# A spectral transformer block: moving the first stage's statistics, corrections, low parts and shift sums between engines

## The chip, the cores and the metric

The kernel runs on one core of one Trainium2 chip. A core has the matrix engine TensorE (PE in the profile, its weight loads PEld), VectorE (DVE), ScalarE (ACT), GpSimd (POOL) and SyncE (SP, which here only issues transfers), each with its own queue of instructions worked off in order, and 16 DMA engines. The metric is device time in microseconds (us) of one execution. A kernel's time is the median of several runs; the profile is of one execution.

## The reference, cut to what matters

```python
mod = (_silu(c) @ w_mod).reshape(c.shape[0], 6, 1, -1)
sa, ca, ga, sb, cb, gb = (mod[:, 0], mod[:, 1], mod[:, 2], mod[:, 3], mod[:, 4], mod[:, 5])
h = _layernorm(x, axis=-1) * (1 + ca) + sa
x = x + ga * _A_ref(h, A_w_r, A_w_i)      # rfft2 over (2048, 512), times complex weights, irfft2
h = _layernorm(x, axis=-1) * (1 + cb) + sb
x = x + gb * _B_ref(h, B_w1, B_b1, B_w2)  # 512 -> 1376, Mish, 1376 -> 512
```

`x` is 1 x 2048 x 512 in float32, `c` is 1 x 512, `w_mod` 512 x 3072. `ca` is called the scale here and `sa` the shift; both are sums over the 512 rows of `w_mod`.

## The kernel before

The 2048 rows are 16 tiles of 128 partitions; tile n holds the rows with index n modulo 16. Three stages follow one another: the forward transform along both axes (the *first stage*, lines 274 to 340), the products with the spectral weights (line 521 on), and the inverse transform with the two dense layers (line 694 on). The order of the instructions on every engine is the order of the program text, written out by hand (`tc.manual_schedule()`). The change is almost wholly in the first stage.

**Start of the first stage.** TensorE runs 14 products of ones (`warm`, L272). ScalarE's queue loads `c` and the scale's part of `w_mod` (`wmc`, two transfers of 512 KB, L277), SP's queue everything else: the transposed tile `xring`, the constants `kr`, the tile `x` and the column matrices `mraw` of tile 0, and then the same three for each tile. The scale sums (`scale_sums`, L238) are 16 products of `wmc` with the gated `c`, in two halves with 4 more warming products between them. VectorE makes the scaled row constants `krs` from them (`scale_rows`, L243, four instructions). The row products with ones give `kb` (`row_sums`, copied by ScalarE at L207), which takes the mean out later.

**Per tile n.** Layernorm's division is put off until after the row transform:

- `norm_sums` (VectorE, L107 and L108): mean and variance of the tile.
- `p1_scale`, for two tiles at a time: epsilon is added on VectorE (L113), ScalarE makes a first guess of the reciprocal root by a logarithm and an exponential (L114, L115), and four small instructions correct it by one Newton step (L129 to L132), on GpSimd except for the first tiles.
- `p1_split`: ScalarE rounds the column matrix to its high part (L188), GpSimd subtracts for the low part (L189) and negates the imaginary halves (L190). It runs three tiles ahead.
- `p1_row` (TensorE, L196): the row products of the transposed tile with `krs`, two tiles ahead of the column products.
- `p1_mean`: VectorE takes the mean out (L211), ScalarE scales by the reciprocal root and rounds (the high part `gh`, L213).
- `p1_low` (VectorE, L219): the low part `gl`, the scaled tile minus `gh`.
- `p1_col` (TensorE, L227 to L229): three trios of products, matrix high x `gh`, matrix low x `gh`, matrix high x `gl`.
- `p1_save` (ScalarE, L233): the result leaves its bank.

The buffers of `gh` and `gl` (tags `g1`, `g2`) are two each, those of the mean-free tile two for each parity, and those of tag `t` two.

**End of the first stage.** The shift sums (`shift_sum`, L248 and L250) run at tiles 10 to 13: ScalarE scales one part of `wms`, GpSimd adds it up. Before the last column product TensorE turns the sum into columns (`mod_columns`, L99); after it come the shift's row products (`shift_rows`, L259) and then the next stage's transposes (L424).

Later stages use `norm_stats` and `norm_scale` for the second layernorm, with the same guess and correction (`norm_refine`, L118 to L124, all on VectorE).

Of the kernel before, what the change touches and what calls it, by code (L numbers as in the profile page):

```python
# [26 lines left out]
def tile_spectral_block(ctx: ExitStack, tc: tile.TileContext, x_d, w1_d, b1_d, w2_d,  # L27
# [40 lines left out]
    nmr = base.tile([P, N2], F32, name="nmr")  # L68

# [40 lines left out]
    def norm_guess(lo, hi):  # L110
        ve = small.tile([P, 4], F32, name="ve")[:, 0:hi - lo]
        r = rstd[:, lo:hi]
        nc.vector.tensor_scalar(ve, mv[:, lo:hi, 1], EPS, None, op0=ALU.add)  # L113
        nc.scalar.activation(r, ve, AF.Ln)  # L114
        nc.scalar.activation(r, r, AF.Exp, scale=-0.5)  # L115
        return ve

    def norm_refine(lo, hi, ve):  # L118
        r = rstd[:, lo:hi]
        nc.vector.tensor_tensor(ve, ve, r, op=ALU.mult)  # L120
        nc.vector.tensor_tensor(ve, ve, r, op=ALU.mult)
        nc.vector.tensor_scalar(ve, ve, -0.5, 1.5, op0=ALU.mult, op1=ALU.add)
        nc.vector.tensor_tensor(r, r, ve, op=ALU.mult)
        nc.vector.scalar_tensor_tensor(nmr[:, lo:hi], mv[:, lo:hi, 0], -1.0, r, op0=ALU.mult, op1=ALU.mult)  # L124

    def p1_scale(lo, hi, eng):
        ve = norm_guess(lo, hi)
        r = rstd[:, lo:hi]
        eng.tensor_tensor(ve, ve, r, op=ALU.mult)  # L129
        eng.tensor_tensor(ve, ve, r, op=ALU.mult)  # L130
        eng.tensor_scalar(ve, ve, 0.5, -1.5, op0=ALU.mult, op1=ALU.add)
        eng.tensor_tensor(r, r, ve, op=ALU.mult)  # L132

    def norm_scale(lo, hi):
        norm_refine(lo, hi, norm_guess(lo, hi))
# [73 lines left out]
    def p1_mean(n):  # L209
        c = buf("hy"[n % 2])  # L210
        nc.vector.scalar_tensor_tensor(c, kb, mv[:, n, 0:1], st.pop(("pg", n)), op0=ALU.mult, op1=ALU.subtract)  # L211
        gh = buf("g1", F32R)
        nc.scalar.activation(gh, c, AF.Copy, scale=rstd[:, n:n + 1])  # L213
        st["g", n] = c, gh

    def p1_low(n):
        c, gh = st.pop(("g", n))
        gl = buf("g2", F32R)
        nc.vector.scalar_tensor_tensor(gl, c, rstd[:, n:n + 1], plain(gh), op0=ALU.mult, op1=ALU.subtract)  # L219
        st["g", n] = gh, gl  # L220
# [25 lines left out]
    def shift_sum(k):  # L246
        t = macc if k == 0 else buf("t")
        nc.scalar.activation(t, wms[:, k, :], AF.Copy, scale=sc[:, k:k + 1])  # L248
        if k:
            nc.gpsimd.tensor_tensor(macc, macc, t, op=ALU.add)  # L250

# [22 lines left out]
    with tc.manual_schedule():  # L274
# [21 lines left out]
        for k in range(4):  # L296
            scale_sums((k,), cps)
            if k == 1:
                warm(4)
# [583 lines left out]
```

## Time and profile before

| what | before |
|---|---|
| runs | 414.62, 415.5, 417.48 us; median 415.5 |
| profiled execution | 414.65 us, of which span 412.7 us |
| TensorE clock granted | 0.999 of full, mean |
| busy, share of the span | PE 96%, PEld 83%, DVE 47%, ACT 35%, POOL 21% |
| first stage | about 0 to 60 us |

The span is what the profile shows; about 2 us of the execution lie around it. A timeline row gives the start, the duration, the engine, the line, the operation, what it writes and reads, the tile's shape and, in brackets, how long the engine stood idle before it and what ended that. "x8" is a merged run of like instructions. A row of one line's instructions gives the count and the shortest, median and longest duration in ns, and the first and last start. A row of waits gives who waited for whom, microseconds in total, how many times and the longest. Matmuls are pipelined: the start of the next says more than the duration. A matmul in float32 stands as two instructions.

### The profile page before, as it was taken

Reading aid. Unit: us, or ns where it says so; the run is one execution under the profiler, and the core shown is the slowest. Engines: PE = TensorE matmul, PEld = TensorE weight load, DVE = VectorE, ACT = ScalarE, POOL = GpSimd, SP = SyncE. Lnnn points to the kernel's source line nnn. Section 1 sums busy time; section 2 is a strip of 40 time slices with the busy share of each in tenths; the row PEclk is TensorE's granted clock in tenths of the full one; section 3 lists DMA queues with packets and bytes.
Section 4 is the critical chain, followed back from the end, with each engine's and each line's share of the span. In section 5 each row is a group of like instructions: output and inputs, shape, how many; then the busy total and the mean of one; then the engine's idle time right before and its main releaser. Section 6 shows DMA issues by size and latency. Waiting matters only on the chain.

```text
span 412.7 us, 5968 instructions
## 1 busy us (share of the span) xinstructions
PE 397.7 (96%) x2287; PEld 343.1 (83%) x2287; DVE 192.1 (47%) x377; ACT 146.3 (35%) x322; POOL 87.6 (21%) x139
## 2 busy tenths in 40 slices
PE   8799979999999999899999999999999999999996
PEld 8798867999899998688878888878888878888874
DVE  2798847787337697553421442311432312422213
ACT  2466844667734752633411222310232310111110
POOL 0467745666214354312100000000000000000000
PEclk9999999999999999999999999999999999999999
DMA  8999790464302223111000200000200000200002
GB/s 294 378 355 320 210 302 6 128 219 162 97 6 83 76 63 87 49 51 29 18 0 2 102 0 2 0 2 0 102 2 0 0 2 0 102 2 1 0 2 102
DMA packets 20316, 34.59 MB, mean 84 GB/s; under 512 B 3648, under 2 KB 6496, under 8 KB 19904
## 3 DMA queue, kind: packets, MB, share of 16 engines
q1 hardware_dynamic: 19856, 33.16, 24.3%
q10 hardware_dynamic: 432, 1.05, 0.7%
q8 instruction: 18, 0.29, 0.3%
q14 instruction: 10, 0.08, 0.1%
HBM read 30.01 MB, written 4.19 MB: 83 GB/s over the span
## 4 chain that ended last, share of the span: by engine, by line
PE 87%; DVE 4%; POOL 3%; issue 2%; ACT 1%; DMA 1%; POOLq 0%
PE bank L664 30%; PE bank L685 29%; PE bank L627 4%; PE bank L617 4%; PE bank L618 3%; PE bank L440 3%; PE bank L486 3%; PE bank L593 2%; PE bank L473 2%; PE bank L272 2%; PE bank L424 1%; PE bank L196 1%; POOL mring L189 1%; DVE buf L456 1%; POOL mring L190 1%
## 5 line engine op out<-in xcount | busy, mean ns | idle before, releaser
L685 PE MATMUL bank<-w,ah 128*128 128x512 f32 (+1 forms) x352 | 108.7, 390 | 1.4 <-issue 1.4
L664 PE MATMUL bank<-h,w1h 128*128 128x512 f32 (+1 forms) x352 | 96.8, 398 | 0.0
L672 ACT ACTIVATE mw<-bank,b1n 128x512 f32<-128x512 f32 (+1 forms) x44 | 30.2, 688 | 181.6 <-PE bank L664 129.1
L673 DVE CAST ah<-mw 128x512 fp32r<-128x512 f32 (+1 forms) x44 | 20.1, 457 | 156.9 <-ACT mw L672 156.9
L685 PEld LDWEIGHTS bank<-w,ah 128*128 128x128 f32 (+1 forms) x352 | 66.1, 188 | 16.1 <-issue 1.8
L664 PEld LDWEIGHTS bank<-h,w1h 128*128 128x128 f32 (+1 forms) x352 | 65.0, 187 | 15.1
L685 PE MATMUL bank<-w,al 128*128 128x512 f32 (+1 forms) x176 | 68.6, 390 | 0.0
L664 PE MATMUL bank<-h,w1l 128*128 128x512 f32 (+1 forms) x176 | 48.2, 396 | 0.0
L664 PEld LDWEIGHTS bank<-h,w1l 128*128 128x128 f32 (+1 forms) x176 | 32.9, 187 | 8.1
L685 PEld LDWEIGHTS bank<-w,al 128*128 128x128 f32 (+1 forms) x176 | 33.0, 188 | 7.4 <-DVE al L674 0.4
L674 DVE TENSOR_TENSOR al<-mw,ah 128x512 fp32r<-128x512 f32 (+1 forms) x44 | 30.4, 692 | 4.5 <-DVE ah L673 0.5
L227 PE MATMUL bank<-buf,mring 128*128 128x512 f32 x48 | 20.8, 433 | 6.4 <-ACT buf L213 3.9
L617 PE MATMUL bank<-kc,d 128*128 128x128 f32 x128 | 24.8, 276 | 0.5 <-ACT d L349 0.5
L618 PE MATMUL bank<-kc,d 128*128 128x128 f32 x128 | 24.7, 275 | 0.0
L107 DVE BATCH_NORM_STATS2 st<-x 128x6 f32<-128x512 f32 x32 | 22.0, 687 | 3.2 <-DMA x<-in_A_x_dram 2.8
L640 POOL TENSOR_TENSOR buf<-buf,modr 128x512 f32<-128x512 f32 (+1 forms) x11 | 14.2, 1287 | 33.5 <-DMA buf<-in_B_w_dram 27.8
L573 POOL TENSOR_TENSOR w1l<-buf,w1h 128x512 fp32r<-128x512 f32 (+1 forms) x12 | 14.4, 1201 | 27.3 <-ACT w1h L572 27.3
L617 PEld LDWEIGHTS bank<-kc,d 128*128 128x128 f32 x128 | 19.4, 192 | 0.7 <-ACT d L349 0.7
L618 PEld LDWEIGHTS bank<-kc,d 128*128 128x128 f32 x128 | 19.4, 192 | 0.0
L189 POOL TENSOR_TENSOR mring<-mraw,mring 128x256 fp32r<-128x256 f32 x16 | 13.9, 867 | 18.0 <-ACT mring L188 18.0
L627 PE MATMUL bank<-kiv,buf 128*128 128x128 f32 x128 | 17.2, 277 | 0.0
L196 PE MATMUL bank<-modr,xring 128*128 128x128 f32 x128 | 16.9, 276 | 0.0
(141 smaller groups left out, 550.0 us busy)
## 6 DMA issues: line engine op xcount, KB each, us to landing
buf<-in_B_w_dram SPq DMA_DIRECT2D x18, 256.0 KB, 2.7
xring<-in_x_t_dram SPq DMA_DIRECT2D x16, 256.0 KB, 5.0
x<-in_A_x_dram SPq DMA_DIRECT2D x16, 256.0 KB, 5.3
wm<-in_w_mod_dram SPq DMA_DIRECT2D x16, 256.0 KB, 4.4
out_dram<-x SPq DMA_DIRECT2D x16, 256.0 KB, 2.1
mraw<-in_km_dram SPq DMA_DIRECT2D x16, 128.0 KB, 5.0
wqa<-in_w_q_dram SPq DMA_DIRECT2D x8, 256.0 KB, 4.3
wqb<-in_w_q_dram SPq DMA_DIRECT2D x8, 256.0 KB, 5.6
```

The lines of the kernel that those rows point to most:

```text
L107: nc.vector.bn_stats(t, x[:, n, :])
L189: nc.gpsimd.tensor_tensor(m[:, 1, 0:256], mraw[:, n, :], plain(m[:, 0, 0:256]), op=ALU.subtract)
L196: nc.tensor.matmul(pgv[:, j], data(j), krs[:, j, :].rearrange("p (c q) -> p c q", c=2), start=True, stop=True)
L227: nc.tensor.matmul(pa, m[:, a, 0:128], g, start=(i == 0), stop=False)
L617: nc.tensor.matmul(o, dj[:, 0:128], kc[0][:, n, :], start=True, stop=False)
L618: nc.tensor.matmul(o, dj[:, 64:192], kc[1][:, n, :], start=False, stop=True)
L627: nc.tensor.matmul(px[:, j * P:(j + 1) * P], e[:, j * P:(j + 1) * P], kiv[:, j, :], start=True, stop=True)
L664: nc.tensor.matmul(ps, w[:, k, fs], h[:, k, :], start=(i == 0), stop=(i == 11))
L672: nc.scalar.activation(w, ps, AF.Mish, bias=b1n[:rows, g % NF:g % NF + 1])
L673: nc.vector.tensor_copy(ah, w)
L674: nc.vector.tensor_tensor(al, w, plain(ah), op=ALU.subtract)
L685: nc.tensor.matmul(out_ps[b][j], a[:, j * P:(j + 1) * P], w2[f // 6][:rows, f % 6, w, :], start=(f == 0 and i == 0), stop=(f == NF - 1 and ...
```

## The change

Line numbers in this section and the diff are the changed kernel's own where they are new.

- The scale's part of `w_mod` is loaded in four transfers of 256 KB: parts 1 and 3 on ScalarE's queue, parts 0 and 2 on SP's, after the transposed tile 0 and ahead of `kr` and tile 0's `x`. The warming products before the scale sums are 11 instead of 14, and the 4 between their halves are gone.
- Tile 0's statistics stand after the scale sums in the text; on VectorE they are ahead of the scaled row constants, as before, but its correction comes after these.
- Epsilon comes in as ScalarE's bias in the logarithm (a tile `eps`), so L113 goes. The correction is three `scalar_tensor_tensor` instructions instead of four, all on VectorE, in the later stages too (where the fifth, for `nmr`, stays).
- Statistics run four tiles ahead of the column products instead of three, and the guess and the correction of a pair are split: the guess at odd n, the correction at the next even n, between the mean step of tile n + 1 and the low part of tile n.
- Odd tiles: ScalarE scales into a plain tile of tag `t`, copies that to `gh`, and GpSimd subtracts for `gl`. Even tiles stay as they were (VectorE makes `gl`).
- The shift sums are four VectorE instructions (`mod_step`), two at n = 12 and two at n = 13; the columns are taken before column product 14 instead of 15.

On VectorE the order of an even n in the steady part is: mean step of n + 1, three correction steps for n + 2 and n + 3, low part of n, statistics of n + 4; of an odd n: mean step of n + 1, statistics of n + 4. On GpSimd an even n has the odd low part of n + 1, then the split of n + 3. On ScalarE an odd n ends with the guess, after the saving of n - 1, the high part of n + 1 and the split of n + 3.

```diff
     def norm_guess(lo, hi):
-        ve = small.tile([P, 4], F32, name="ve")[:, 0:hi - lo]
         r = rstd[:, lo:hi]
-        nc.vector.tensor_scalar(ve, mv[:, lo:hi, 1], EPS, None, op0=ALU.add)
-        nc.scalar.activation(r, ve, AF.Ln)
+        nc.scalar.activation(r, mv[:, lo:hi, 1], AF.Ln, bias=eps)
         nc.scalar.activation(r, r, AF.Exp, scale=-0.5)
...
+    def norm_refine(lo, hi, sign):
         r = rstd[:, lo:hi]
...
+        t = small.tile([P, 4], F32, name="ve")[:, 0:hi - lo]
+        for out, a, one, op in ((t, mv[:, lo:hi, 1], EPS, ALU.add), (t, t, -0.5 * sign, ALU.mult),
+                                (r, t, 1.5 * sign, ALU.add)):
+            nc.vector.scalar_tensor_tensor(out, a, one, r, op0=op, op1=ALU.mult)
...
     def p1_mean(n):
         c = buf("hy"[n % 2])
         nc.vector.scalar_tensor_tensor(c, kb, mv[:, n, 0:1], st.pop(("pg", n)), op0=ALU.mult, op1=ALU.subtract)
-        gh = buf("g1", F32R)
-        nc.scalar.activation(gh, c, AF.Copy, scale=rstd[:, n:n + 1])
-        st["g", n] = c, gh
+        one = rstd[:, n:n + 1]
+        if n % 2:
+            g, c = c, buf("t")
+            nc.scalar.activation(c, g, AF.Copy, scale=one)
+        gh, gl = buf("g1", F32R), buf("g2", F32R)
+        if n % 2:
+            nc.scalar.copy(gh, c)
+            nc.gpsimd.tensor_tensor(gl, c, plain(gh), op=ALU.subtract)
+        else:
+            nc.scalar.activation(gh, c, AF.Copy, scale=one)
...
-        for k in (0, 2):
-            nc.scalar.dma_start(wmc[:, k:k + 2, :], wm_d[:, 1, k:k + 2, :])
+        load_scale(nc.scalar, 1)
+        load_scale(nc.scalar, 3)
         nc.scalar.preload_act_table_set("natural_log_exp_and_others")
         load_xt(0)
+        load_scale(nc.sync, 0)
+        load_scale(nc.sync, 2)
         nc.sync.dma_start(kr, kr_d)
...
-        warm(14)
-        norm_sums(0)
-        p1_scale(0, 1, nc.vector)
+        warm(11)
         cps = [bank(t) for t in "DDCC"]
         for k in range(4):
             scale_sums((k,), cps)
-            if k == 1:
-                warm(4)
+        norm_sums(0)
+        norm_guess(0, 1)
         scale_rows(cps)
+        norm_refine(0, 1, -1)
...
         norm_sums(1)
-        p1_scale(1, 2, nc.gpsimd)
         p1_mean(0)
+        norm_guess(1, 2)
+        norm_refine(1, 2, -1)
         p1_split(1)
+        p1_mean(1)
+        p1_low(0)
         p1_split(2)
+        norm_sums(2)
+        norm_sums(3)
+        norm_guess(2, 4)
         for n in range(N2):
...
-            if n + 1 < N2:
+            if 1 <= n and n + 1 < N2:
                 p1_mean(n + 1)
-            p1_low(n)
-            if n == N2 - 1:
+            if n and n % 2 == 0 and n + 2 < N2:
+                norm_refine(n + 2, n + 4, -1)
+            if n:
+                p1_low(n)
+            if n == N2 - 2:
                 shift_columns()
             p1_col(n)
             if n + 3 < N2:
                 p1_split(n + 3)
+            if n + 4 < N2:
+                norm_sums(n + 4)
             if n == 0:
-                norm_sums(2)
-            if n + 3 < N2:
-                norm_sums(n + 3)
-                if n % 2 == 0:
-                    p1_scale(n + 2, n + 4, nc.gpsimd if n else nc.vector)
-            if 10 <= n < 14:
-                shift_sum(n - 10)
+                norm_refine(2, 4, -1)
+            if n % 2 and n + 3 < N2:
+                norm_guess(n + 3, n + 5)
+            if n in (12, 13):
+                for k in (2 * n - 24, 2 * n - 23):
+                    mod_step(macc, wms[:, k, :], k, nc.vector)
```

More of the change, by code (lines that the diff above doesn't have):

```diff
@@ L68, in tile_spectral_block @@
     nmr = base.tile([P, N2], F32, name="nmr")
+    eps = base.tile([P, 1], F32, name="eps")
     saz = base.tile([P, NQ], F32, name="saz")
@@ L244, in scale_rows @@
                                            op0=ALU.mult, op1=ALU.add)
[L246 to L250, printed above, removed]
     def shift_columns():
@@ L285, in tile_spectral_block @@
         nc.vector.memset(ones, 1.0)
+        nc.vector.memset(eps, EPS)
         nc.vector.memset(b1n[:, NF - 1:NF], 0.0)
```

31 lines of the change are left out of this document (12 added, 19 removed).

## The prediction

> **What bounds the kernel now.** I read the page's engine table first, then who waited for whom on TensorE in the first stage (0 to 62 us), then the timeline of that stage, engine by engine.
>
> ```profile
> span 412.7 us, 5968 instructions
> PE 397.7 (96%) x2287; PEld 343.1 (83%) x2287; DVE 192.1 (47%) x377; ACT 146.3 (35%) x322; POOL 87.6 (21%) x139
> ...
> PE bank L227 <- ACT buf L213: 3.9, 6, 2.1
> PE bank L227 <- DVE buf L219: 2.5, 2, 2.3
> ```
>
> TensorE is busy 96% of the span, so a change can only win where it waits. Those waits stand in the first stage, at the column products (L227), behind the scaled tile (L213) and its low part (L219). The change touches that stage, so I take its clock on TensorE.
>
> ```profile
> 16.79 1.05 PE L196 MATMUL bank<-modr,xring 128*128 128x128 f32 x8
> ...
> 21.63 1.05 PE L196 MATMUL bank<-modr,xring 128*128 128x128 f32 x8
> 22.44 0.47 PE L227 MATMUL bank<-buf,mring 128*128 128x512 f32 x1
> ...
> 23.93 1.05 PE L196 MATMUL bank<-modr,xring 128*128 128x128 f32 x8
> 24.74 0.47 PE L227 MATMUL bank<-buf,mring 128*128 128x512 f32 x1
> ...
> 27.11 0.48 PE L227 MATMUL bank<-buf,mring 128*128 128x512 f32 x1
> ...
> 28.60 1.05 PE L196 MATMUL bank<-modr,xring 128*128 128x128 f32 x8
> ...
> 49.48 1.05 PE L196 MATMUL bank<-modr,xring 128*128 128x128 f32 x8
> ...
> 56.65 1.05 PE L99 MATMUL bank<-ones,modr 128*128 128x1 f32 x8 [0.39 <-POOL modr L250]
> 57.56 0.48 PE L227 MATMUL bank<-buf,mring 128*128 128x512 f32 x1
> ...
> 59.95 2.27 PE L424 MATMUL bank<-ident,a_sb 128*128 128x128 f32 x15
> ```
>
> Every column product is followed at once by the row product (L196) two tiles on, so the start of that row is the column's end. One column product takes 22.44 to 23.93 = 1.49 us (three trios), a row product 0.81 to the next column. Two tiles without a stall take 27.11 - 22.44 = 4.67. Column 4 ends at 28.60 and column 12 at 49.48: four pairs in 20.88, or 5.22 each, so 0.55 of stall per pair. From column 12 to the transposes of the next stage (59.95) are 10.47 us, with work for 0.81 + 3 x 1.49 + 0.91 (L99) + 0.90 (shift rows, 59.95 - 57.56 - 1.49) = 7.1. The next stages have full TensorE, so I let whatever the transposes gain reach the end.
>
> **The start.**
>
> ```profile
> GB/s 294 378 355 320 210 302 6 128 219 162 97 6 83 76 63 87 49 51 29 18 0 2 102 0 2 0 2 0 102 2 0 0 2 0 102 2 1 0 2 102
> ...
> 6.44 1.95 PE L238 MATMUL bank<-sc,wmc 128*128 128x128 f32 x16
> ...
> 7.53 0.69 DVE L107 BATCH_NORM_STATS2 st<-x 128x6 f32<-128x512 f32 x1 [2.79 <-DMA x<-in_A_x_dram]
> 8.22 1.05 PE L272 MATMUL bank<-ones 128*128 128x128 f32 x8
> ...
> 9.12 1.95 PE L238 MATMUL bank<-sc,wmc 128*128 128x128 f32 x16
> ...
> 10.44 1.18 DVE L243 SCALAR_TENSOR_TENSOR modr<-kr,bank 128x128 f32<-128x128 f32 x4 [0.23 <-PE bank L238]
> ...
> 13.09 0.59 ACT L207 COPY modr<-bank 128x512 f32<-128x512 f32 x1 [3.70 <-PE bank L196]
> ...
> 13.71 1.40 DVE L211 SCALAR_TENSOR_TENSOR buf<-modr,mv,bank 128x512 f32<-128x512 f32 x2 [1.08 <-ACT modr L207]
> ...
> 14.49 0.72 ACT L213 ACTIVATE buf<-buf,rstd 128x512 fp32r<-128x512 f32 x1 [0.47 <-DVE buf L211]
> ```
>
> Today TensorE runs 14 warming products, half of the scale sums (6.44), 4 warming products, and the other half (9.12); the scaled constants follow 1.32 behind. The change takes out 3 + 4 warming products; four of them take 9.12 - 8.22 = 0.90, so the scale sums would start 0.68 earlier, at 5.76. A half takes 8.22 - 6.44 = 1.78, so the second would start at 7.54 and L243's successor at 8.86, if the data are there. The four parts go two on each queue, and on SP's queue parts 0 and 2 stand ahead of kr and tile 0's x. First rows, parts, kr and x are 7 x 0.26 = 1.84 MB. By the page's slices of 10.3 us (294 and 378 GB/s) 3.03 MB have passed at 10.3, so 1.84 MB at about 7.2. Today x landed at 7.53 with weights still to come; now all of them go ahead of it or beside it. I take 8.1, an estimate between 7.5 and 9.4; the parts themselves are ahead of kr and x and then in time for TensorE. VectorE's queue now has tile 0's statistics (0.72 + 0.18) ahead of the scaled constants (27.73 to 28.45 below, and its own 0.18), so x sets them: 9.05. From there to the first mean is 13.71 - 10.44 = 3.27, which gives K = 12.3; I take 12.4 for the correction steps now behind the constants. The two more issues on SP's queue come ahead of every later load; these are spaced by the transfers, whose bytes are the same, so they cost nothing more. Gain 1.3 (bounds 0, if x lands at 9.4, and 1.6, if TensorE sets it).
>
> **VectorE, GpSimd and ScalarE per pair.**
>
> ```profile
> 26.40 0.71 DVE L211 SCALAR_TENSOR_TENSOR buf<-modr,mv,bank 128x512 f32<-128x512 f32 x1
> 27.06 0.75 DVE L219 SCALAR_TENSOR_TENSOR buf<-buf,rstd 128x512 fp32r<-128x512 f32 x1
> 27.73 0.69 DVE L107 BATCH_NORM_STATS2 st<-x 128x6 f32<-128x512 f32 x1
> 28.45 0.18 DVE L108 BATCH_NORM_AGGREGATE mv<-st 128x2 f32<-128x6 f32 x1
> 28.67 0.26 DVE L113 TENSOR_SCALAR ve<-mv 128x2 f32<-128x2 f32 x1
> 28.84 0.74 DVE L211 SCALAR_TENSOR_TENSOR buf<-modr,mv,bank 128x512 f32<-128x512 f32 x1
> ...
> 30.88 0.18 DVE L108 BATCH_NORM_AGGREGATE mv<-st 128x2 f32<-128x6 f32 x1
> 30.98 0.71 DVE L211 SCALAR_TENSOR_TENSOR buf<-modr,mv,bank 128x512 f32<-128x512 f32 x1
> ```
>
> VectorE works without a gap here: 30.98 - 26.40 = 4.58 a pair. The change takes out one low part (0.67) and the epsilon addition (0.17), and adds three correction steps. Without these it needs 2 x 0.66 (means) + 0.67 + 2 x 0.72 + 2 x 0.10 (statistics) = 3.63. What the three cost depends on who else is in the memory:
>
> ```profile
> 18.24 0.73 POOL L189 TENSOR_TENSOR mring<-mraw,mring 128x256 fp32r<-128x256 f32 x1
> 18.32 0.67 DVE L129 TENSOR_TENSOR ve<-ve,rstd 128x2 f32<-128x2 f32 x1 [0.51 <-ACT rstd L115]
> 19.03 0.16 DVE L130 TENSOR_TENSOR ve<-ve,rstd 128x2 f32<-128x2 f32 x1
> 19.06 0.41 POOL L190 TENSOR_SCALAR mring<-mring 128x256 fp32r<-128x256 f32 x1
> 19.22 0.27 DVE L131 TENSOR_SCALAR ve<-ve 128x2 f32<-128x2 f32 x1
> ...
> L573 POOL TENSOR_TENSOR w1l<-buf,w1h x12: 932/1274/1611, 121.1 to 156.9; 128x512 fp32r<-128x512 f32 x8, 128x352 fp32r<-128x352 f32 x4
> L189 POOL TENSOR_TENSOR mring<-mraw,mring x16: 722/736/1199, 9.5 to 51.0; 128x256 fp32r<-128x256 f32 x16
> L190 POOL TENSOR_SCALAR mring<-mring x16: 405/407/809, 10.3 to 52.3; 128x256 fp32r<-128x256 f32 x16
> ```
>
> A step of 0.16 on two columns, with two operands in SBUF, took 0.67 and ended 0.02 after GpSimd's operation did; the next slipped in, and the third ended with GpSimd's next one. So a correction costs 3 x 0.19 = 0.57 beside an idle GpSimd, and about 1.1 beside a busy one (rest of one operation, one short operation, 0.3 of its own). GpSimd will be busy: it loses four steps of 0.2 and gets the odd tile's low part, 1.27 by the median of L573, the same form: 1.27 + 2 x (0.74 + 0.41) + five gaps of 0.08 = 4.0 a pair, and what it waits itself comes on top. I take 1.1, so VectorE's pair is 3.63 + 1.1 = 4.73 against TensorE's 4.67; the bounds are 4.20 and 5.8 (a correction that starts with the 1.27 ahead of it). ScalarE gets one more copy per pair, 0.59 by the nearest row (13.09); TensorE waits for it only through the chain that follows. Two waits are new in queues: GpSimd's subtraction waits for ScalarE's copy with the split of three tiles on behind it, which has three tiles of time; ScalarE's logarithm waits for the second tile's statistics with the next column's saving behind it, which frees a bank of two. Statistics four tiles ahead want x sooner: a tile's three loads are 0.66 MB, 1.8 us at 378 GB/s, against 2.3 us per tile, and x of tile 4 is due 7.2 after x of tile 0, at 15.3, wanted at K+5.6 = 18.
>
> [...]
>
> **The walk through the first columns,** from K, in queue order. ScalarE ends the high part of tile 0 at K+1.5 (13.71, 14.49 and 0.72) and then has tile 1's logarithm and exponential (0.51 with the waits, by the row of 18.32; to 1.86); VectorE's correction of tile 1 waits for these, and behind it stand mean 1 (to 3.11) and low part 0 (to 3.9). So column 0 ends at K+4.5, where it took to K+3.1 before (16.79): statistics have moved, but one wait is new. The odd low part on GpSimd (ScalarE's scale and copy to 4.53, then 1.27) is there at 5.85, and column 1 ends at K+6.9 (21.63, K+7.9, before). Then statistics 2, 3 (to 5.6), 4 (6.4), correction 2-3 (7.2), mean 2 and its high part: column 2 starts at K+8.7, as before. Statistics 5, mean 3, correction 4-5 (10.45) and low part 2 (11.2) end column 2 at K+11.8 (before K+10.2); column 3 at 14.1; statistics 6 and 7, means 4 and 5, correction 6-7 and low part 4 (16.0) end column 4 at K+16.6, against 28.60 - 13.71 = 14.9. Loss 1.7 (bounds 0.8 with no collision, 3.2 with three).
>
> **Columns 4 to 12:** four pairs at 4.75, 19.0 instead of 20.88. Gain 1.9 (bounds 2.2, TensorE's 4.67, and -2.4).
>
> **The end.** The shift sums leave ScalarE and GpSimd (with the 0.39 wait at L99) and become four VectorE steps of 0.7 (of L219's kind and shape), two of them ahead of mean 14 and two ahead of mean 15. From low part 12 at time e: 4 x 0.7 + 0.66 and 0.3 for one collision = e+3.8; L99 moves ahead of column 14 and waits for it, 0.91 to e+4.75, column 14 to 6.25. Mean 15, scale, copy and GpSimd's subtraction, 0.66 + 0.72 + 0.6 + 1.27 + 0.1, are ready at e+7.2, so column 15 ends at 7.75 and the transposes start at e+8.65. Column 12, whose last trio takes some 0.55, ends at e+0.55: 8.1 against 10.47. Gain 2.4 (bounds 3.3 and 1.4). The fused correction of the later stages lies beside full TensorE: 0; without that cover it would save one step of 0.2 at five places. L99's other neighbours, the memset and the bias operand cost nothing that anyone waits for.
>
> **Sum.** 1.3 - 1.7 + 1.9 + 2.4 = 3.9. The profiled execution took 414.65 (span 412.7), 0.85 under the median of 415.5 and with the fastest run: 414.65 - 3.9 = 410.75; I say 410.7.
>
> **Rivals.**
> - *No collisions.* GpSimd's gaps let the corrections through: column 4 at K+15.7, pairs at 4.67, VectorE ahead by the end: 1.3 - 0.8 + 2.2 + 3.3 = 6.0, 408.65. Against it: GpSimd is loaded 4.0 of 4.7.
> - *The steady pairs stay at 5.22,* since a correction falls behind the long subtraction: 1.3 - 1.7 + 0 + 2.4 = 2.0, 412.65.
> - *All three steps wait,* GpSimd being back ahead of the second too: one operation (0.41 to 0.73) more per correction, 0.5 with its gap, at three in the walk and four later: 3.9 - 3.5 = 0.4, 414.25. For it: 19.03 and 19.06 stand only 0.03 apart. [...]
> - *Late start.* x lands at 9.4 or later behind four parts: 2.6, 412.05. Before, x landed at 7.53.
> - *Slower: GpSimd becomes the bound* with the subtraction. At the longest it has taken, 1.61 + 2 x (1.20 + 0.81) + 0.4 = 6.0 a pair, six pairs from K+4.5 to column 12: 52.9 + 8.65 - 0.55 = 61.0, 1.1 later than before: 415.75. It turns the sign from 5.85 a pair on; typical values give 4.0.
>
> [...]
>
> **Chances.** Forecast 0.45, no collisions 0.25, pairs at 5.22 0.14, three waits 0.07, late start 0.05, GpSimd bound 0.04. The range 408.2 to 412.7 leaves out the cases at 414.25 and 415.75 and the edges. A measurement of this kernel tells about 1% (4.15 us) from no change. Faster by more than that: the free case and some six tenths of the forecast's spread, 0.52; within 1%: 0.45; slower by more: 0.03.
>
> **What would show it.** The first scaled-constant step near 9.0 and waiting for x or the statistics, not TensorE; the first mean near 12.4; column 0's last trio waiting for VectorE's low part by 1.4; correction steps of 0.16 stretched to 0.4 to 0.7; pairs of 4.7 to 4.8 at L228; L99 waiting for VectorE's shift sum; transposes near 56.1. Wrong would be corrections at 0.19 throughout (then the free case), or TensorE waiting for GpSimd's low part in most pairs.

## The result and the profile after

The changed kernel takes 414.33 us (median of 20 runs, 412.37 to 416.04), the kernel before 415.92 (20 runs, 414.62 to 417.95): a ratio of 0.995 with the interval 0.9931 to 0.9968. It is faster, by half a per cent; the forecast was 410.7 us, 1.2% under the 415.5 known at that time. Executions of one kernel lie some 3 us apart, in part along with TensorE's mean clock (last section); hence the intervals.

The profiled execution took 413.91 us. First its page, then who waited for whom on TensorE (what waits, for what: us in all, times, longest).

```profile
span 411.7 us, 5922 instructions
...
PE 397.0 (96%) x2273; PEld 342.7 (83%) x2273; DVE 192.1 (47%) x374; ACT 151.0 (37%) x326; POOL 86.0 (21%) x116
```

```profile
PE bank L228 <- DVE buf L221: 2.7, 2, 1.7
PE bank L695 <- issue: 2.4, 1, 2.4
PE bank L100 <- DVE modr L95: 1.4, 1, 1.4
PE bank L228 <- ACT buf L213: 1.2, 2, 0.8
```

The waits at the column products (L228, L227 before) are 3.9 us instead of 6.4. Two others stand beside them: one at the shift's column sums (L100; 0.4 before, at L99) and one some 115 us later at the first down product (L695; 1.4 before, at L685). Now TensorE's timeline of the first stage.

```profile
16.92 0.50 PE L228 MATMUL bank<-buf,mring 128*128 128x512 f32 x1 [1.67 <-DVE buf L221]
...
29.16 1.05 PE L188 MATMUL bank<-modr,xring 128*128 128x128 f32 x8
...
48.05 1.05 PE L188 MATMUL bank<-modr,xring 128*128 128x128 f32 x8
...
51.88 1.05 PE L100 MATMUL bank<-ones,modr 128*128 128x1 f32 x8 [1.36 <-DVE modr L95]
52.80 0.48 PE L228 MATMUL bank<-buf,mring 128*128 128x512 f32 x1
...
54.02 0.63 PE L228 MATMUL bank<-buf,mring 128*128 128x512 f32 x1
...
54.87 0.63 PE L228 MATMUL bank<-buf,mring 128*128 128x512 f32 x1
...
57.23 1.05 PE L254 MATMUL bank<-kr,cols 128*128 128x128 f32 x8
58.12 2.04 PE L434 MATMUL bank<-ident,a_sb 128*128 128x128 f32 x13
```

Row products again mark column ends: column 4 at 29.16, column 12 at 48.05, the transposes at 58.12. With K, the first mean step, from VectorE's timeline of the start (8.43 tile 0's statistics, 9.26 the scaled constants, 12.49 the first mean):

```profile
8.43 0.69 DVE L108 BATCH_NORM_STATS2 st<-x 128x6 f32<-128x512 f32 x1 [3.81 <-DMA x<-in_A_x_dram]
...
9.26 1.15 DVE L244 SCALAR_TENSOR_TENSOR modr<-kr,bank 128x128 f32<-128x128 f32 x4
...
12.49 0.75 DVE L203 SCALAR_TENSOR_TENSOR buf<-modr,mv,bank 128x512 f32<-128x512 f32 x1 [0.17 <-ACT modr L199]
```

| stretch (us) | before | forecast | after |
|---|---|---|---|
| K | 13.71 | 12.4 | 12.49 |
| K to the end of column 4 | 14.89 | 16.6 | 16.67 |
| columns 4 to 12 | 20.88 | 19.0 | 18.89 |
| column 12 to the transposes | 10.47 | 8.1 | 10.07 |
| transposes to the first down product | 108.51 | as before | 109.32 |

Three of five steps came out within 0.11 us; the last two lost 2.0 and 0.8 of the 3.9 us forecast.

What happened at the end of the stage stands on VectorE and GpSimd. VectorE first: low part 12, then the shift sums.

```profile
46.68 0.74 DVE L221 SCALAR_TENSOR_TENSOR buf<-buf,rstd 128x512 fp32r<-128x512 f32 x1
47.35 0.47 DVE L93 TENSOR_SCALAR modr<-wms,sc 128x512 f32<-128x512 f32 x1
47.85 1.85 DVE L95 SCALAR_TENSOR_TENSOR modr<-wms,sc,modr 128x512 f32<-128x512 f32 x1
...
50.28 1.54 DVE L95 SCALAR_TENSOR_TENSOR modr<-wms,sc,modr 128x512 f32<-128x512 f32 x2
```

GpSimd beside it:

```profile
47.89 1.27 POOL L211 TENSOR_TENSOR buf<-buf 128x512 fp32r<-128x512 f32 x1 [1.13 <-DMA wqa<-in_w_q_dram]
```

The first sum with two operands in SBUF takes 1.85 us, from 47.85 on, where the two at 50.28 take 1.54 together: 1.1 too much, the length of GpSimd's subtraction less a little. TensorE waits for the sums, and right after that wait its clock is halved. Busy time and granted clock (the column of 1.00 and 0.50) of two stretches:

```profile
50.13:53.55 3.42, 2.06 (x15) 1.80 (x14) 3.30 (x6) 2.14 (x4) 1.07 (x2) 1.00 0.89 293
53.55:56.96 3.41, 3.41 (x13) 3.03 (x12) 0.00 (x0) 1.06 (x3) 1.28 (x1) 0.50 0.99 330
```

For 3.41 us TensorE never idles and runs at half clock: column products follow each other at 54.87 - 54.02 = 0.85 instead of 0.47.

The second loss, in the row stage. The kernel before, GpSimd scaling the first slab of w2 (L640) and TensorE's first down product:

```profile
150.42 1.27 POOL L640 TENSOR_TENSOR buf<-buf,modr 128x512 f32<-128x512 f32 x1 [1.51 <-DMA buf<-in_B_w_dram]
...
168.46 0.70 PE L685 MATMUL bank<-w,ah 128*128 128x512 f32 x2 [1.41 <-issue]
```

The same of the kernel after, with VectorE's split of the fourth slab (L657) and tile 15's statistics (L108) behind it:

```profile
149.58 1.28 POOL L650 TENSOR_TENSOR buf<-buf,modr 128x512 f32<-128x512 f32 x1 [2.58 <-DMA buf<-in_B_w_dram]
...
150.91 1.20 DVE L121 SCALAR_TENSOR_TENSOR ve<-ve,rstd 128x4 f32<-128x4 f32 x1
...
162.31 0.69 DVE L657 TENSOR_TENSOR w<-buf,w 128x512 fp32r<-128x512 f32 x1 [0.78 <-ACT w L656]
162.91 0.69 DVE L108 BATCH_NORM_STATS2 st<-x 128x6 f32<-128x512 f32 x1
...
167.44 0.70 PE L695 MATMUL bank<-w,ah 128*128 128x512 f32 x2 [2.42 <-issue]
```

The transposes came 1.83 earlier, the first slab only 0.84, and the down product 1.02: TensorE waits 2.42 instead of 1.41. Beside it a small correction step of tiles 8 to 11 took 1.20 instead of 0.16. I took that step for the cause at first; the runs say otherwise. "First slab" means from here on GpSimd's scaling of it, which starts when its transfer has landed.

### The profile page after: what moved, and what is told of

The parts are those of the page before. It is cut to its first block, busy times and chain, and to the rows that moved or that the text cites. A ratio compares the mean times of both kernels' runs of the same rounds, so it can differ in the third digit from the quotient of the medians.

```text
span 411.7 us, 5922 instructions
## 1 busy us (share of the span) xinstructions
PE 397.0 (96%) x2273; PEld 342.7 (83%) x2273; DVE 192.1 (47%) x374; ACT 151.0 (37%) x326; POOL 86.0 (21%) x116
## 4 chain that ended last, share of the span: by engine, by line
PE 85%; DVE 8%; ACT 2%; DMA 1%; issue 1%; SPq 0%; POOL 0%; POOLq 0%
PE bank L674 30%; PE bank L695 29%; PE bank L627 4%; PE bank L637 4%; PE bank L628 3%; PE bank L450 3%; PE bank L496 3%; PE bank L603 2%; PE bank L483 2%; DMA x<-in_A_x_dram 1%; PE bank L188 1%; PE bank L434 1%; PE bank L228 1%; DVE buf L466 1%; DVE buf L203 1%
## 5 line engine op out<-in xcount | busy, mean ns | idle before, releaser
L695 PE MATMUL bank<-w,ah 128*128 128x512 f32 (+1 forms) x352 | 108.7, 390 | 2.4 <-issue 2.4
L695 PEld LDWEIGHTS bank<-w,ah 128*128 128x128 f32 (+1 forms) x352 | 66.1, 188 | 17.0 <-issue 2.8
L695 PE MATMUL bank<-w,al 128*128 128x512 f32 (+1 forms) x176 | 68.6, 390 | 0.0
L695 PEld LDWEIGHTS bank<-w,al 128*128 128x128 f32 (+1 forms) x176 | 33.0, 188 | 7.4 <-DVE al L684 0.4
L228 PE MATMUL bank<-buf,mring 128*128 128x512 f32 x48 | 21.8, 455 | 3.9 <-DVE buf L221 2.7
L108 DVE BATCH_NORM_STATS2 st<-x 128x6 f32<-128x512 f32 x32 | 22.0, 687 | 4.2 <-DMA x<-in_A_x_dram 3.8
L640 DVE TENSOR_TENSOR x<-x,bank 128x512 f32<-128x512 f32 x16 | 10.8, 674 | 13.0 <-PE bank L637 13.0
```

What stands on the lines that cost most here:

```text
L108: nc.vector.bn_stats(t, x[:, n, :])
L228: nc.tensor.matmul(pa, m[:, a, 0:128], g, start=(i == 0), stop=False)
L695: nc.tensor.matmul(out_ps[b][j], a[:, j * P:(j + 1) * P], w2[f // 6][:rows, f % 6, w, :], start=(f == 0 and i == 0), stop=(f == NF - 1 and ...
```

## The experiments

Two theories to begin with. L: a VectorE step with two operands in SBUF is held up by a GpSimd operation that runs beside it (0.67 us for 0.16 in the kernel before, at 18.32), and this is what the change pays at three places (the first stage's corrections, the shift sums, the later corrections). C: the wait at L100 brings the clock down. All runs are compared with the kernel before on the same chip; the kernel after stands at 0.995.

**Filling the wait at L100** (the kernel after):

```
             if n == N2 - 2:
+                warm(6)
                 shift_columns()
```

> The changed kernel with six more warming products between column product 13 and the shift sum's columns; their result is not used. Theory C (the clock): TensorE stood idle for 1.36 us there and then ran products of one column, and 1.6 us later its clock fell to half for 3.4 us, which stretched columns 14 and 15 from 2.98 to 4.43. If so, the six products (0.225 us each, 1.35 in all) fill the stall without delaying anything, the records show no half clock near 53 us, columns 14 and 15 take about 3.0, the transposes start near 56.7 instead of 58.12 and the time falls by about 1.4 us (some runs of the changed kernel show more than one such stretch, so it may be up to 2). Rival S (the stall alone): the half clock is chance or comes from something else; then the stretch stays, and the time is the changed kernel's.

Measured: 413.73 us, ratio 0.9916 (0.9881 to 0.995). TensorE's timeline:

```profile
51.93 1.05 PE L100 MATMUL bank<-ones,modr 128*128 128x1 f32 x8
52.85 0.48 PE L228 MATMUL bank<-buf,mring 128*128 128x512 f32 x1
...
56.00 1.05 PE L254 MATMUL bank<-kr,cols 128*128 128x128 f32 x8
56.89 1.39 PE L435 MATMUL bank<-ident,a_sb 128*128 128x128 f32 x8
```

L100 starts at the same time, and the columns behind it need 56.00 - 52.85 = 3.15 instead of 4.43: no half clock in this profile (granted 1.00 from 50.1 to 57.0), transposes 1.23 earlier, span 410.6. That fits C, but one profile does not show it. The gain in the medians is smaller and its interval touches 0.995: the profiled execution is the only one of nine with a mean clock of 1.00, the other eight have 0.995 or 0.996, and where their clock fell is not known. The eleven profiles of the kernel after and its variants say more. In five L100 waits 1.32 to 1.36 us: three fall to half clock there (column products 0.85 apart), with 10.05 to 10.07 us from column 12 to the transposes, and two do not, with 8.74 and 8.77. In the six where the wait is filled or 0.80 and less, none falls. So in these eleven the fall at this place stands only behind the long wait, and not always; it costs 1.3 us.

**The first stage's guess in PSUM:** logarithm and exponential write a bank, so that each correction step reads one operand from SBUF; the same at the other guesses and corrections.

```
+        gps = bank("D")
-        norm_guess(2, 4)
+        norm_guess(2, 4, gps)
...
-                norm_refine(2, 4, -1)
+                norm_refine(2, 4, -1, gps)
```

> The changed kernel, but in the first stage the guess of the reciprocal root from tile 1 on is written to a PSUM bank, so each correction step reads only one operand from SBUF; the result is the same. [...] Then the steps take 0.16 to 0.25 each, a correction 0.6 to 0.75 instead of about 1.1, column 4 ends near K+15.8 instead of K+16.67 (K is the first mean), pairs take 4.67 instead of 4.73, VectorE reaches the shift sums some 0.8 us earlier relative to column 12, and the transposes start 1 to 2.5 us earlier than in the changed kernel. [...]

Measured: 410.85 us, ratio 0.9845 (0.9803 to 0.9887). The correction steps of the kernel after, seven of each (shortest/median/longest ns):

```profile
L121 DVE SCALAR_TENSOR_TENSOR ve<-mv,rstd x7: 373/554/671, 19.2 to 45.7; 128x2 f32<-128x2 f32 x7
L121 DVE SCALAR_TENSOR_TENSOR ve<-ve,rstd x7: 160/160/161, 19.7 to 46.3; 128x2 f32<-128x2 f32 x7
L121 DVE SCALAR_TENSOR_TENSOR rstd<-ve,rstd x7: 252/255/256, 19.9 to 46.5; 128x2 f32<-128x2 f32 x7
```

And with the guess in PSUM:

```profile
L121 DVE SCALAR_TENSOR_TENSOR ve<-mv,bank x7: 123/156/157, 18.8 to 43.7; 128x2 f32<-128x2 f32 x7
L121 DVE SCALAR_TENSOR_TENSOR ve<-ve,bank x7: 156/157/158, 19.0 to 43.9; 128x2 f32<-128x2 f32 x7
L121 DVE SCALAR_TENSOR_TENSOR rstd<-ve,bank x7: 156/157/158, 19.1 to 44.1; 128x2 f32<-128x2 f32 x7
```

The stretch is gone, with nothing moved: the first step takes 0.156 us instead of 0.554, by the medians. Column 4 ends at K+15.09 instead of K+16.67, columns 4 to 12 take 18.34 (46.18 - 27.84), and the transposes start at 54.40. This is the free case of the prediction, made by hand; L holds for the first stage.

**The later guess in PSUM,** in the bank pool that the transposes of the next stage use too:

```
     def norm_scale(lo, hi):
-        norm_guess(lo, hi)
-        norm_refine(lo, hi, 1)
+        g = bank("D")
+        norm_guess(lo, hi, g)
+        norm_refine(lo, hi, 1, g)
```

> The changed kernel, but in the later stage (the second layernorm) the guess lies in a PSUM bank; the first stage is as in the changed kernel. [...]

Measured: 416.13 us, ratio 0.9973 (0.9943 to 1.0002). The edit made a wait of its own: the transposes of h waited 2.2 us for the bank (L604 for L121). The mean clock of this execution is 0.990, against 0.996 in the kernel after; whether it fell behind that wait is not shown. It tells nothing on L.

**The shift sums accumulated in PSUM:**

```
-                    mod_step(macc, wms[:, k, :], k, nc.vector)
+                    nc.vector.scalar_tensor_tensor(macc if k == 3 else mps, wms[:, k, :], one, mps,
+                                                   op0=ALU.mult, op1=ALU.add)
```

> The changed kernel, but the four shift steps add up in a PSUM bank and only the last writes SBUF; the result is the same. [...] Rival: the shift steps are not what the columns wait for (mean 15 and the chain to GpSimd's last subtraction are), then columns 14 and 15 only wait elsewhere and the gain is under 0.4.

Measured: 412.7 us, ratio 0.9898 (0.9862 to 0.9933). VectorE's timeline:

```profile
48.69 0.76 DVE L354 SCALAR_TENSOR_TENSOR bank<-wms,sc,bank 128x512 f32<-128x512 f32 x1
```

The sum that took 1.85 takes 0.76. From column 12 to the transposes it is 56.56 - 48.62 = 7.94 us, near the 8.1 of the prediction; L100 waits 0.53 instead of 1.36, and the column products behind it stand 0.47 apart, not 0.85. L holds for the sums.

**The later correction in the old form,** with the epsilon added on VectorE:

```
     def norm_scale(lo, hi):
-        norm_guess(lo, hi)
-        norm_refine(lo, hi, 1)
+        nc.vector.tensor_scalar(ve, mv[:, lo:hi, 1], EPS, None, op0=ALU.add)
...
+        nc.vector.tensor_tensor(r, r, ve, op=ALU.mult)
```

> The kernel after with the correction of the later stage (the row stage and the guess for each later batch) in the form of the kernel before: epsilon added on VectorE, two products, one scalar step, one product. The first stage stays fused. In the kernel after TensorE's first down product waits 2.42 us (1.41 before), and the correction of tiles 8 to 11 has steps of 0.73 and 1.20 us that start within GpSimd's L650 and L583. Theory L (these steps have two operands in SBUF and stand still beside GpSimd; it is the moment, not the form, that decides): the old form meets the same two GpSimd instructions, two of its products are stretched to 0.6 to 1.2 us again, the down product waits 2.0 to 2.6 and the time stays at that of the kernel after, within 0.5 us (ratio 0.995 to 0.997). Rival F (the fused form itself is what costs: three steps of two operands in a row instead of two): the stretch falls below 0.7 us in sum, the wait goes back to 1.4 and the kernel is 1.0 us faster than the kernel after (ratio 0.9925).

Measured: 412.93 us, ratio 0.9888 (0.987 to 0.9906): the expectation of L missed, and its rival F (the form itself costs, 0.9925) is the nearer one. In its profile the steps ran at 0.16 each and the down product waited 1.01. From the transposes to the down product are 108.10 us, as in the kernel before (108.51) and not as in the kernel after (109.32). The traces show what the form does, ahead of the first slab of w2, where VectorE and GpSimd each subtract with two operands in SBUF (GpSimd's row is two instructions). The kernel before:

```profile
146.29 2.62 POOL L573 TENSOR_TENSOR w1l<-buf,w1h 128x352 fp32r<-128x352 f32 x2 [1.42 <-ACT w1h L572]
146.46 1.31 DVE L609 TENSOR_TENSOR h<-buf,h 128x512 fp32r<-128x512 f32 x1
```

The kernel after:

```profile
144.28 0.69 DVE L619 TENSOR_TENSOR h<-buf,h 128x512 fp32r<-128x512 f32 x1
144.30 2.70 POOL L583 TENSOR_TENSOR w1l<-buf,w1h 128x352 fp32r<-128x352 f32 x2 [1.43 <-ACT w1h L582]
```

Before, GpSimd starts first and VectorE is stretched, 1.31 for 0.69. After, the fused corrections have made VectorE 0.35 earlier against the transposes (86.16 behind them instead of 86.51). It starts 0.02 ahead of GpSimd, and GpSimd's first subtraction takes 1.46 instead of 0.94. The transfer of the first slab is issued when that one is over: 87.67 us behind the transposes instead of 87.30. This holds in every profile but that of the run with the wait for a bank. The four with the old later correction take 2.61 or 2.62 for the two subtractions and have the first slab at 90.1 to 90.5; the nine with the fused one take 2.68 to 2.70 and have it at 91.1 to 92.4. The issue stands at 87.30 and 87.32 in two of the four (the kernel before, the old later correction), and at 87.66 or 87.67 in four of the nine (the kernel after, the first run of three edits together, the split behind the statistics, the three edits that held).

**The guess of tiles 8 to 11 alone, in a free bank:**

```
+        g = bank("C") if lo == 8 else None
```

> The kernel after with the guess of tiles 8 to 11 alone (the correction with the steps of 0.73 and 1.20 us) in a PSUM bank that nothing else uses at that time (tag C, not D, which the transposes of the batches needed in the run before). Theory L (a step with one operand in SBUF does not wait for GpSimd): all three steps take 0.16 to 0.2 us, the chain behind them comes 1.5 us earlier, the down product waits 0.9 to 1.5 us instead of 2.42, and the time is 1.0 us below that of the kernel after: 413.3 beside 414.3, ratio 0.9925. Rival E (the wait of the down product comes from the activation chain behind it, ACT's table load, Mish and the cast beside GpSimd, and not from the correction): the steps take 0.16 and the wait stays above 2.2 us, the time stays (ratio 0.995).

Measured: 414.76 us, ratio 0.9933 (0.9911 to 0.9955): no gain that can be told. VectorE's timeline:

```profile
148.85 0.16 DVE L121 SCALAR_TENSOR_TENSOR ve<-mv,bank 128x4 f32<-128x4 f32 x1 [0.52 <-ACT bank L114]
...
149.43 1.19 DVE L127 SCALAR_TENSOR_TENSOR nmr<-mv,rstd 128x4 f32<-128x4 f32 x1
```

The three steps take 0.16 each, and the next step with two SBUF operands takes 1.19 in their place; the down product waits 2.16 (2.46 in the run with the filled wait, whose transposes start at the same time).

**Three edits together** (first guess, sums, tiles 8 to 11):

> Three edits in one: the guess of the first stage in PSUM, the shift sums accumulated in PSUM, and the guess of tiles 8 to 11 in PSUM. The first alone gave 0.9845, the second alone 0.9898, against 0.995 for the kernel after. Theory L, if the gains lie at different places and reach the end: pairs of 4.6 us (as with the first alone), the last stretch of the first stage 7.4 to 8.0 us from column 12 to the transposes, the down product's wait 0.9 to 1.6; in sum 2.6 + 0.7 + 1.0 below the kernel after with the first alone counted once: 409.0 us, ratio 0.979 to 0.982. Rival B (what the first stage gains is given back where TensorE waits in the later stage, because that chain is bound by transfers and not by TensorE): the down product waits 2.5 us or more and the time stays at that of the first alone, 410.8, ratio 0.984.

Measured: 412.0 us, ratio 0.9874 (0.9855 to 0.9894). The transposes start at 54.86, the corrections are nearly free, and the down product waits 2.66: rival B. So the stretch of these steps is not what holds it. GpSimd's first slab in this run:

```profile
146.65 1.27 POOL L659 TENSOR_TENSOR buf<-buf,modr 128x512 f32<-128x512 f32 x1 [2.93 <-DMA buf<-in_B_w_dram]
```

Here stood the clue. From this start to the down product (164.43) are 17.78 us; in the kernel before 168.46 - 150.42 = 18.04, after 167.44 - 149.58 = 17.86. Over the ten profiles with this order of the stage (the run with the wait for a bank left out) it is 17.72 to 18.04, while the stretch of the corrections in between goes from 0.06 to 2.1 us. What differs is when the first slab has landed: 90.1 to 92.4 us behind the transposes, and that goes with the form of the later correction (above).

**One part undone: odd low parts on VectorE as the even ones.**

```
-        if n % 2:
-            nc.scalar.copy(gh, c)
-            nc.gpsimd.tensor_tensor(gl, c, plain(gh), op=ALU.subtract)
-        else:
-            nc.scalar.activation(gh, c, AF.Copy, scale=one)
+        nc.scalar.activation(gh, c, AF.Copy, scale=one)
```

> One part of the change undone: the low parts of odd tiles are made as those of even tiles, by one fused step on VectorE (L221) instead of a second copy on ScalarE and a subtraction on GpSimd. The pairs of columns 4 to 12 then load VectorE with one step of 0.74 us more: in the kernel after VectorE is busy 18.07 of 18.89 us there, or 4.5 of 4.72 a pair. Theory D (VectorE's own work sets the pair; the move to GpSimd is what made the pair 4.7): pairs of 5.2 to 5.4 us, columns 4 to 12 in 21 instead of 18.89, and the time 2.0 to 2.5 us above that of the kernel after: 416.5, ratio 1.000. [...]

Measured: 416.09 us, ratio 0.9956 (0.9935 to 0.9978). Busy time between column 4's and column 12's end (span, then PE, PEld, DVE, ACT, POOL) of this run:

```profile
31.41:50.45 19.04, 19.02 (x139) 17.51 (x138) 18.49 (x44) 13.88 (x32) 9.59 (x17) 1.00 0.91 290
```

And of the kernel after:

```profile
29.16:48.05 18.89, 18.89 (x138) 17.53 (x137) 18.07 (x41) 16.56 (x37) 13.94 (x21) 1.00 0.99 335
```

My theory D falls: four steps of 0.75 more on VectorE, and the pairs stay at 4.76. The first and third correction steps shrink from 0.60 and 0.26 to 0.29 and 0.18 on average, the last stretched sum from 1.85 to 1.1. In the pairs, moving the low parts to GpSimd takes 3.0 us of steps off VectorE, and its busy time falls only from 18.49 to 18.07: the steps stretched beside GpSimd take most of it back. It counts elsewhere: here column 4 ends at K+18.06 (31.41 - 13.35) instead of K+16.67, with a wait of 2.05 for column 1's low part, while column 12 to the transposes takes 8.41 instead of 10.07, with 0.71 of wait at L100 and no half clock.

What held the pairs stands in the kernel before: ScalarE's scaling (L213), for which TensorE waits there, itself waited for the last step of GpSimd's correction (us in all, times).

```profile
  POOL rstd L132: 9.1, 6
```

In the kernel after, with the correction on VectorE, that line waits for VectorE's mean step alone.

**The split of w2 behind the statistics** (the kernel after):

```
-        if s >= 13:
-            split_w2(s - 13)
         if s >= 1:
             norm_sums(s - 1)
...
+        if s >= 13:
+            split_w2(s - 13)
```

> The kernel after with one thing moved in the row stage: the splitting of a slab of w2 (L656 on ScalarE, L657 on VectorE) is issued behind the statistics of the tile instead of ahead of them. In the kernel after the statistics of tile 15 stand on VectorE behind L657, which starts at 162.31 after 0.78 of waiting for a slab that GpSimd could only scale once its transfer had landed (L650 at 160.33 after 1.57 for the DMA); the tile itself is added by 161.5. Theory W (the down product waits for the chain slab, statistics of tile 15, guess, table load, Mish; the stretched corrections only make the slabs later): the statistics start at 161.5 instead of 162.91, the guess and Mish follow, the down product waits 1.0 to 1.2 us instead of 2.42 and the time is 1.2 to 1.4 below that of the kernel after: ratio 0.992 instead of 0.995. Rival V (the chain is held by Mish's table load and by the up products, not by the statistics): wait and time stay, ratio 0.995.

Measured: 411.66 us, ratio 0.9871 (0.9833 to 0.991): theory W, and more of it than expected. VectorE (third slab, then tile 15's statistics) and TensorE:

```profile
158.91 0.69 DVE L657 TENSOR_TENSOR w<-buf,w 128x512 fp32r<-128x512 f32 x1 [0.29 <-ACT w L656]
...
160.23 0.69 DVE L108 BATCH_NORM_STATS2 st<-x 128x6 f32<-128x512 f32 x1
```

```profile
164.78 0.70 PE L695 MATMUL bank<-w,ah 128*128 128x512 f32 x2 [0.67 <-PE bank L674]
```

The statistics no longer stand behind the fourth slab; from the transposes (57.20) to the down product are 107.58 us instead of 109.32, although two correction steps are stretched to 1.14 and 1.20 in this profile.

**The three edits that held, together:** first guess and sums in PSUM, split behind the statistics.

> The guess of the first stage in PSUM (0.9845 by itself), the shift sums accumulated in PSUM (0.9898 by itself, 0.995 without), and the splitting of w2 behind the statistics. If the three places are separate: pairs of 4.6, transposes 7.6 us after column 12, and the down product waits about 1.2 instead of the 2.66 us that it waited when the first stage was shortened without this: 409.2 us beside the kernel after's 414.3, ratio 0.980 to 0.983. Rival: slabs of w2 come at the pace of their two buffers (2.6 us each), so that the down product or a later one waits for a slab instead, and the time stays at 410.5 to 412, ratio 0.984 to 0.988.

Measured: 407.32 us (406.84 to 408.22), ratio 0.9764 (0.9728 to 0.9801), faster than both kernels and than expected. The transposes start at 54.19, the down product at 161.16 without a wait, and the granted clock is 0.9 or more in all 40 slices of its page; all six runs have a mean clock of 0.998 or more.

**The start alone, on the kernel before:** four transfers on two queues, 11 filling products.

```
-        for k in (0, 2):
-            nc.scalar.dma_start(wmc[:, k:k + 2, :], wm_d[:, 1, k:k + 2, :])
+        load_scale(nc.scalar, 1)
+        load_scale(nc.scalar, 3)
...
+        load_scale(nc.sync, 0)
+        load_scale(nc.sync, 2)
```

> The kernel before with one part of the change alone: the scale's weights in four transfers, two on the queue of ScalarE and two on SyncE's, and 11 instead of 14 + 4 filling products. The prediction put the start's gain at 1.3 us (first mean step at 12.4 instead of 13.71), of which a third came from the shorter first step. If the transfers make it, the first mean step stands at 12.4 to 12.8, column 4 ends 0.9 to 1.3 us earlier, the pairs stay at 5.22, and the time falls by 0.9 to 1.3 us (ratio 0.997 to 0.998) if the earlier transposes reach the end, less if the later stage gives it back. Rival S (x and the transposed tile land later instead, the gain of the start comes from the order of the statistics): the first mean step at 13.5 or later, ratio 1.000.

Measured: 415.97 us, ratio 0.9968 (0.9944 to 0.9992). VectorE's timeline:

```profile
10.14 0.50 DVE L132 TENSOR_TENSOR rstd<-rstd,ve 128x1 f32<-128x1 f32 x1
10.57 1.28 DVE L243 SCALAR_TENSOR_TENSOR modr<-kr,bank 128x128 f32<-128x128 f32 x4
```

The scale sums are over by 10.2, yet the constants wait for VectorE's old order, statistics and correction first, and K is 13.94. The ratio says a little gain; by the profile the transfers alone do not make it, and need the constants ahead of the correction.

**The split behind the statistics, on the kernel before:**

> The kernel before with the splitting of a slab of w2 issued behind the statistics of the tile, as in the run on the kernel after that gained by it. In twelve profiles with the old order the down product starts 17.7 to 18.0 us after GpSimd begins to scale the first slab of w2, whatever stands between; with the new order 15.7. If the hold behind the slab is older than the change (theory W), the kernel before gains too, but no more than it waits: the down product's wait of 1.41 us falls to 0 to 0.7 and the time by 0.7 to 1.4 us (ratio 0.9966 to 0.9983). Rival (the hold was made by the change's earlier transposes alone, the 1.41 of before being the activation chain): ratio 1.000, the wait stays above 1.2.

Measured: 417.07 us, ratio 0.9996 (0.9968 to 1.0023): no gain, theory W missed here. (Its text counts twelve profiles; there are ten.) VectorE's timeline:

```profile
163.17 0.69 DVE L647 TENSOR_TENSOR w<-buf,w 128x512 fp32r<-128x512 f32 x1 [1.01 <-ACT w L646]
...
164.49 0.69 DVE L107 BATCH_NORM_STATS2 st<-x 128x6 f32<-128x512 f32 x1
```

Tile 15 now stands behind the third slab, and this one came late as well; a correction step of 1.31 and the slab's copy (0.60) ahead of the table load (1.28) took the rest. In the two profiles that gained, the first slab is 15.6 and 15.7 us ahead of the down product; here it is 17.87. So the order helped where the third slab was there in time.

## Why the prediction was right or wrong

- **The start, "Gain 1.3": right in this execution, generous as a rule.** x set the constants as forecast (9.26 for 9.05). K follows x's landing by 4.06 (12.49 - 8.43; in the first run of three edits together 13.80 - 9.73 = 4.07), and by 4.06 to 4.24 in nine of eleven profiles with this start. In the other two (the old later correction, the low parts on VectorE) x lands earlier, at 8.16 and 7.75, the constants wait for the scale sums, and K is 13.60 and 13.35. All eleven have K from 12.49 to 13.80, 12.99 on average, two with the old start 13.71 and 14.19. About 1.0 rather than 1.3.
- **The walk, "column 4 at K+16.6": right,** with the columns on the way 0.2 to 0.5 us behind their forecast. The working has a slip: 1.5 and 0.51 are 2.0, not 1.86 (tile 1's correction began at K+1.96). The run with the guess in PSUM shows that 1.6 of its length is the stretched correction steps and what they push.
- **"Columns 4 to 12 … 19.0": right in size, not in the reason given.** I credited the low part taken off VectorE. The run that gives it back has 19.04. What shortened the pairs is the correction that left GpSimd, by the wait of 9.1 us for it that is gone; it was not tried apart from the statistics four tiles ahead and the epsilon addition that went. The bound of 4.67 for a pair without a stall was too long: with the guess in PSUM a pair takes 18.34 / 4 = 4.59.
- **"The end … 8.1": wrong, 10.07.** "0.3 for one collision" was the mis-sized term: the sum met GpSimd's subtraction of 1.27 nearly from its beginning, so it cost 1.1. With a first step of 0.47 for 0.7 that makes 0.6 of the 2.0 lost. The clock was not in the working at all and makes the rest: 10.07 - (56.89 - 48.13) = 1.3 us, by the run with the filled wait. The sums in PSUM gave the forecast stretch, 7.94.
- **"I let whatever the transposes gain reach the end": wrong, 0.8 lost.** I looked for full TensorE and not for what paces the engines beside it. The first slab landed only 0.84 earlier with the transposes 1.83 earlier, and from there to the down product it takes 17.7 to 18.0 us in ten profiles, wherever the transposes start.
- **"The fused correction of the later stages lies beside full TensorE: 0": wrong, and it is what lost those 0.8.** TensorE does cover the saved steps themselves: from the transposes to the down product no other wait of it is longer than 0.5 us, before or after. But they bring VectorE ahead of GpSimd at the last splits of w1, and that holds up the first slab. With the old later correction the stretch is 108.10. The stretch of the corrections at tiles 8 to 11 is only a companion, since GpSimd's scaling slides onto them: freeing them gained nothing.

The rival "all three steps wait" named nearly this time, 414.25, but not what happened: the second step takes 0.160 in all seven corrections.

What stays open is the rest of the first slab's delay. Of the 0.99 (91.46 instead of 90.47 behind the transposes), 0.37 is the later issue; from issue to use the transfer takes 3.8 us instead of 3.2. The four profiles named above with the late issue take 3.7 to 4.2, the two others 3.2 and 2.8. In the kernel after, the first run of three edits together and the split behind the statistics a packet of the instruction queue (0.02 MB) passes in the same window, and the transfer ends in a tail of mostly 15 to 40 GB/s; in the kernel after it is 18 GB/s over some 0.9 us. The run with the old later correction has no such packet in its window, the kernel before has it 0.9 us ahead of the slab, and neither has a tail under 50 GB/s of more than 0.3 us. That the packet holds up the transfer is argued from these windows, not tried.

## What to carry to other kernels

TensorE at 96% hid nothing by itself here: of the 1.83 us that the transposes gained, 1.02 reached the first down product. So ask for each gain what paces the engines beside it up to the point where TensorE next waits, here slabs that come through two buffers. A step saved beside it is not free of effect either: it moves its engine against the others, and here it made VectorE the first, by 0.02 us, at a place where GpSimd's work had to be over sooner. Price a VectorE step with two SBUF operands by the longest GpSimd operation it can meet (here 1.85 us for 0.77, beside one of 1.27), and before moving work between the two put one operand in PSUM: for the first stage's corrections that was worth 1% here on top of the change (0.9845 for 0.995). It was not tried on the kernel before. Where a row of waits is removed, the one that is left may cost more than its length if the clock drops behind it: here 1.36 us of wait, and 1.3 more by the clock.

## What the runs showed of the hardware

- TensorE's granted clock fell to 0.50 for 3.41 us behind a stretch in which it had been busy for 2.06 of 3.42 us, at a cost of about 1.3 us. It is not sure to happen: the run with the later guess in bank C had 2.18 busy of 3.50 at the same place and kept 1.00, and so did the kernel before with 1.20 of 3.40 (51.0 to 54.4). So the busy share alone does not decide it.
- A part of the spread of a kernel's runs goes with that clock: runs with mean clocks of 1.00, 0.996 and 0.992 took 412.41, 413.69 to 415.46, and 416.0 to 416.32 us in one kernel (tiles 8 to 11 in PSUM). Not all of it does: in the kernel after, ten runs at 0.996 lie between 412.37 and 414.78. The fastest version is also the steadiest, 1.4 us from end to end over six runs.
- Of two subtractions with both operands in SBUF, one on VectorE and one on GpSimd, the later one was stretched: 1.31 for 0.69 on VectorE where GpSimd started 0.17 ahead, and 1.46 for 0.94 on GpSimd where VectorE started 0.02 ahead.
